# Two pairs of heads share the mapping and summing of their last 64 tokens, zeros fill idle TensorE for longer, and a regular block is written last

## The chip, the cores and the metric

The kernel runs on one core of a Trainium2 chip. A core has five engines that run side by side and meet at semaphores: TensorE (PE, matrix products into PSUM), VectorE (DVE), ScalarE (ACT), GpSimd (POOL) and SyncE (SP, which here issues all DMAs). PSUM has 8 banks of 512 fp32 columns. The metric is the time of one execution in microseconds.

## The reference, cut to what matters

Three stages follow each other: linear attention with an exponential feature map, a gated convolution with two dense layers, and a gMLP with a spatial product.

```python
# q, k, v: (8, 8, 576, 64), w_phi: (64, 128)
def phi(x):
    proj = einsum('bhsd,df->bhsf', x, w_phi)
    proj = proj - max(abs(proj), axis=-1, keepdims=True)
    return concatenate([exp(proj), exp(-proj)], axis=-1)
q_p, k_p = phi(q), phi(k)
kv  = einsum('bhsf,bhsd->bhfd', k_p, v)
z   = sum(k_p, axis=2)
num = einsum('bhsf,bhfd->bhsd', q_p, kv)
den = einsum('bhsf,bhf->bhs', q_p, z)[..., None] + 1e-06
x   = num / den                      # to (8, 576, 512)
# stage 2: gate = sigmoid(causal conv of x, 5 taps); x = (gate * (x @ w_val)) @ w_out
# stage 3: h = relu(x @ w_in); u, v = halves of h; v normalized over its 512 columns;
#          out = (u * (w_spatial @ v + b_spatial)) @ w_out2
```

## The kernel before, in words

Attention works on 32 pairs of heads (8 batches of 4 pairs). A pair's 128 partitions hold two heads of 64 channels. Its 576 tokens are 512 = 4 x 128 and a tail of 64.

For each pair, `load_k` loads the keys (128x576), the values of 512 tokens, and the values of the tail in two loads, one for each head. `project_k` maps the 512 tokens' keys (the keys are the stationary side, `w_phi` the moving one; both heads run at once on 64 rows of the array each). `project_q` maps the queries and, ahead of them, tokens 448 to 575 of the keys, of whose result only the last 64 rows are used. `kexp` and `kexp_last` take the maximum of the magnitudes and the two exponentials. `kvacc` sums the products of key features and values over tokens: two column tiles of 64 at once for the 512 tokens, then four 64x64 tiles at once for the tail. Each value row carries a column of ones, so the sums of the features come with it (65 columns). `kvout` copies the sums to SBUF. `qmax` takes the maximum over the feature partitions on POOL, `qexp` the exponentials, `weigh` (from the sixth pair on) folds the two halves of the denominator, `num` makes numerators and denominators in four column tiles of 32, and `divide` sends the denominators through DRAM (`rden`), spreads them and multiplies.

`mlp(b)` does the other stages for one batch: values (`val`), convolution and gate, the normalized half (`vchunk`), the other half (`uhalf`), the spatial product (`spatial`) and the output rows (`outrows`). All products there are three fp32r products of high and low parts. The tails of two batches (64 tokens each) share one block of output rows, which the kernel writes in two DMAs.

The order isn't the program's own. Every step is recorded as an operation with a key (a due time, in batches; pairs are 2/8 apart), and `Plan.order` simulates the engines with costs written into the kernel and takes, on each engine, the ready operation with the smallest key. A change of the array's form (full, 64 rows, 64 columns, 32 columns, 64x64) is charged by `MODE`. The constants `AK_...`, `AQ_...`, `W_...` and `M_...` shift the keys of the steps, `WINDOW`, `FA_HOLD` and `RA_HOLD` bound how far an operation may run ahead. Two arenas of SBUF columns (`fa` plain fp32, `ra` fp32r) and the 8 banks are given out along this order; an operation waits until there is room. Where PE is idle in the plan before `FILL` us and a bank has rested, a product of zeros is put in. The resulting order is fixed at build time, and each engine runs its instructions in it.

In the profile, L423 is the line through which all DVE and ACT instructions go, L458 POOL's, L469 the DMAs', L483 the MLP's products (`gemm`), L494 attention's products and the folding of weights (`products`), and L396 the zeros. The program records each fp32 product as two instructions.

Of the kernel before, what the change touches and what calls it, by code (L numbers as in the profile page):

```python
# [14 lines left out]
ACTF = mybir.ActivationFunctionType  # L15
ALU = mybir.AluOpType
# [4 lines left out]
F = 128  # L21
DM = 512
# [6 lines left out]
HALF = S // 2  # L29
TSPLIT = ((0, 256), (256, 320))  # L30
COLS = 29888
FA_COLS = 18368
A_LEAD, A_RATE = 1.6098, 1.0
AK_FIRST, AK_LOAD, AK_PROJ, AK_ACC, AK_SUM, AK_TURN = 2.1681, -0.1666, -0.9481, -1.1792, -0.0975, 0.5005
AQ_LOAD, AQ_PROJ, AQ_MAX, AQ_EXP, AQ_NUM, AQ_HEAD, A_DIV = -0.1281, -3.1984, -0.6423, 0.825, -0.9895, 1.7889, 5.0169
W_VAL, W_CONV, W_OUT, W_G, W_U, W_SP, W_OUT2, W_STEP = -1.0763, -1.0716, -1.6199, -1.783, -1.2251, -0.0604, 0.0451, 0.1666
M_CONV, M_VAL, M_V, M_U, M_SP, M_OUT, M_ALL = -0.2041, -0.309, -0.2989, -0.0525, 0.0418, 0.2823, 57.899
LONG_W, LONG_A, LONG_M = False, False, True
WINDOW = 0.5957
FA_HOLD = 2874  # L40
RA_HOLD = 3444
PA_HOLD = 0
LATER = 0.2441

MODE = 0.2916

EARLY = 5

REST, SOON = 6.0, 150.0
READY = {"PE": 1.0, "ACT": 2.0, "DVE": 0.9, "POOL": 0.6, "SP": 0.75}  # L50
# [12 lines left out]
FLOW, LAND, AFLOAT = 3.9, {"in": 1.4, "out": 0.3, "own": 0.85}, 8  # L63


FILL, RESTED = 60.0, 1.5


class View:
# [303 lines left out]
def attn_moe_gmlp_kernel(  # L373
# [88 lines left out]
    def dma(out, in_, queues=16):  # L462
        shape = out.shape() if isinstance(out, View) else out.shape
        packets = 1
        for d in shape[:-1]:
            packets *= d

        def run():
            nc.sync.dma_start(out=real(out), in_=real(in_))  # L469

        kind = "own" if views(in_) and views(out) else "in" if views(out) else "out"
        if kind == "own" and (in_.buf.dram or out.buf.dram):
            kind = "in" if in_.buf.dram else "out"
        moving = packets * (0.008 + 4 * shape[-1] / 27e3) / queues
        plan.add({"SP": (0.475 if shape[0] == 128 else 0.65, moving, run)}, views(in_), views(out), dma=kind)
# [14 lines left out]
    def products(t, mms, *modes):  # L490

        def run():
            for o, l, r, first, last in mms:
                nc.tensor.matmul(real(o), lhsT=real(l), rhs=real(r), start=first, stop=last)  # L494


        begun = {id(o.buf) for o, _, _, first, _ in mms if first}
        plan.add({"PE": (t, 1.0, run)}, [v for _, l, r, *_ in mms for v in (l, r)] +
                 [o for o, *_ in mms if id(o.buf) not in begun], [o for o, *_ in mms], (modes[0], modes[-1]))

    def psum():
        return pa.buf(512)
# [130 lines left out]
    def load_k(P):  # L633
        b, hp = divmod(P, NP)
        k, v, vr = fa.buf(S), fa.buf(4 * 2 * VW), fa.buf(VW)
        dma(k, kT[b, hp, :, 0:S])
        dma(v.rearrange("p (c d) -> p c d", c=4), v1[b, 0:REM, hp].rearrange("(c p) d -> p c d", p=128))
# [17 lines left out]
        ], ROWS)  # L655
        return kas

    def project_q(k, q):

        qas, rest = ([psum() for _ in range(2)] for _ in range(2))  # L660
        products(2 * 4 * (REM + F + S - REM) / 4800 + 0.13, [
            (rest[hh][:, 0:F], k[half(hh), S - 128:S], wphi[half(hh)], True, True) for hh in range(2)
        ] + [
            (rest[hh][:, F:F + 64], wphi[half(hh)], q[half(hh), REM:S], True, True) for hh in range(2)
        ] + [(qas[hh], wphi[half(hh)], q[half(hh), 0:REM], True, True) for hh in range(2)], ROWS)
        return [r[64:128, 0:F] for r in rest], [(qas[hh], rest[hh][:, F:F + 64]) for hh in range(2)]

    def kexp(acc, n):

# [9 lines left out]
    def kexp_last(accs):  # L679

        m, e = fa.buf(4)[64:128], fa.buf(2 * F)
        for hh, acc in enumerate(accs):
            dve("tensor_reduce", out=m[:, hh:hh + 1], in_=acc, axis=AX.X, op=ALU.max, apply_absolute_value=True)
        dve("tensor_scalar", out=m[:, 2:4], in0=m[:, 0:2], scalar1=-1.0, scalar2=None, op0=ALU.mult)
# [6 lines left out]
    def kvacc(kp, kpl, v, vr):  # L691


        accs, mms = [psum() for _ in range(2)], []
        for hh, acc in enumerate(accs):
            for c in range(4):
                for s in range(2):
                    for j in range(2):
                        mms.append((
                            acc[64 * j:64 * j + 64, DZ * s:DZ * s + DZ],  # L700
                            kp[hh][:, s, F * c + 64 * j:F * c + 64 * j + 64],
                            v[:, 2 * VW * c:2 * VW * c + 2 * VW][:, vcols(hh)], c == s == 0, False,
                        ))
        for s in range(2):
            for j in range(2):
                for hh, acc in enumerate(accs):
                    mms.append((acc[64 * j:64 * j + 64, DZ * s:DZ * s + DZ], kpl[half(hh), s, 64 * j:64 * j + 64],
                                vr[half(hh), hh:hh + DZ], False, s == 1))
        products((4 * 4 + 2) * 4 * DZ / 2400 + 0.3, mms, COLS2, TILES)
        return accs  # L710

    def kvout(accs):

        kv = fa.buf(4 * DZ)
        for hh, acc in enumerate(accs):
            copy(kv[:, 2 * DZ * hh:2 * DZ * hh + 2 * DZ], acc[:, 0:2 * DZ])
        return kv

    def values(kv, s, hh, i):
        o = 2 * DZ * hh + DZ * s + hh + 32 * i  # L720
# [71 lines left out]
    def attention():  # L792
        n = B * NP

        def at(t, sub=0.0):
            plan.key = (t + sub) / 8 * A_RATE - A_LEAD

        for P in range(n):
            t = 2 * P
            first = AK_FIRST if P == 0 else 0.0  # L800
            at(t, AK_LOAD - first)
            k, v, vr = load_k(P)
            at(t, AQ_LOAD - first)
            q = load_q(P)
            at(t, AK_PROJ - first)
            kas = project_k(k)
            at(t, AQ_PROJ - first)
            kls, qas = project_q(k, q)
            at(t, AK_ACC)
            kp = [kexp(a, 4) for a in kas]  # L810
            kpl = kexp_last(kls)
            at(t, AQ_MAX)
            pms = [qmax(a) for a in qas]
            at(t, AK_SUM)
            kva = kvacc(kp, kpl, v, vr)
            at(t, AK_TURN)
            kv = kvout(kva)
            es, ts = [], []
            for hh in range(2):
                at(t, AQ_HEAD * hh + AQ_EXP)  # L820
                es.append(qexp(*pms[hh]))
                at(t, AQ_HEAD * hh + AQ_NUM)
# [3 lines left out]
            at(t, A_DIV)  # L826
            divide(P, nd, dn)


    zrem = []  # L830

    def mlp(b):
# [148 lines left out]
        def outrows(z, places):  # L981
# [4 lines left out]
            copy(ot, acc)  # L986
            n = 128 // len(places)
            for i, (c, t0) in enumerate(places):
                dma(out[c, t0:t0 + n], ot[n * i:n * i + n])

        def outblock(j, o):
            outrows([[t[:, o:o + 128] for t in z] for z in zs[j]], [(b, TSPLIT[j][0] + o)])


        for j in range(2):
# [68 lines left out]
```

## Time and profile before

| | |
|---|---|
| median of 3 runs | 838.4 us (838.19 to 838.61) |
| profiled execution | 836.76 us, its span 835.0 us |
| mean granted clock of TensorE | 0.998 |
| PE busy | 816.7 us, 8240 products |
| DVE, ACT, POOL busy | 653.9, 533.9, 146.7 us |

The span is the time from the first to the last instruction; what the execution takes beyond it lies around it. Busy time of PE is that of overlapping products, so a full row of it doesn't yet say that each product is at its shortest; from one form's first start to the next form's first start is the safer measure. Idle time of an engine costs something only where that engine ends last.

### The profile page before, as it was taken

The page shows a single profiled execution, that of the slowest core. Times are in us where ns is not written, and L with a number is a line of the kernel's source. Part 1 is how long each engine was busy: PE and PEld are TensorE (multiplying, and loading weights), DVE is VectorE, ACT ScalarE, POOL GpSimd, SP SyncE. Part 2 cuts the span into 40 slices and gives each one's busy share as a digit, 9 for nine tenths or more (in the row PEclk, how much of TensorE's full clock was granted, in tenths as well). Part 3 has the DMA queues.
Part 4 walks back from the last instruction along what each step waited for, and adds up shares of the span by engine and source line. Part 5 has one row for each costly group of instructions (what it writes and reads, how often), then busy time and mean ns, then how long its engine had stood idle before and what let it go on. Part 6 is the DMA issues. An engine that isn't in the chain of part 4 may idle for free.

```text
span 835.0 us, 20782 instructions
## 1 busy us (share of the span) xinstructions
PE 816.7 (98%) x8240; PEld 684.1 (82%) x8240; DVE 653.9 (78%) x1583; ACT 533.9 (64%) x1148; POOL 146.7 (18%) x106
## 2 busy tenths in 40 slices
PE   9999699999999999999999999999999999999997
PEld 8455497789888888789788898889888897899896
DVE  5979899999879968598679968699587976586631
ACT  6868868986568647786468745678377754643321
POOL 3224222231213202231013202222022302000000
PEclk9999999999999999999999999999999999999999
DMA  8444513231222202321023212312023210110101
GB/s 289 123 160 142 135 61 117 89 100 40 74 62 73 72 28 62 100 74 57 18 87 90 72 40 59 96 53 72 28 72 92 74 42 29 46 30 13 38 7 64
DMA packets 55479, 62.23 MB, mean 75 GB/s; under 512 B 18259, under 2 KB 34771, under 8 KB 55381
## 3 DMA queue, kind: packets, MB, share of 16 engines
q1 hardware_dynamic: 55380, 60.90, 25.0%
q8 instruction: 65, 1.06, 0.6%
q14 instruction: 34, 0.27, 0.1%
HBM read 50.09 MB, written 9.58 MB: 71 GB/s over the span
## 4 chain that ended last, share of the span: by engine, by line
PE 77%; DVE 9%; ACT 6%; DMA 3%; issue 2%; SPq 1%; POOL 0%; ACTq 0%; DVEq 0%; POOLq 0%
PE bank L483 55%; PE bank L494 22%; DVE fa L423 7%; ACT fa L423 5%; DVE ra L423 1%; DMA fa<-rden 1%; SPq L469 1%; DMA fa<-in_w_spT_dram 1%; DMA fa<-in_w_in_dram 1%; DMA fa<-in_qT_dram 0%; DMA fa<-in_w_val_dram 0%; DMA rden<-fa 0%; ACT ra L423 0%; DVE wg L423 0%; POOL fa L458 0%
## 5 line engine op out<-in xcount | busy, mean ns | idle before, releaser
L423 ACT ACTIVATE fa<-fa 128x576 f32<-128x576 f32 (+3 forms) x413 | 260.5, 682 | 76.6 <-DVE fa L423 66.3
L423 ACT ACTIVATE fa<-bank 128x512 f32<-128x512 f32 (+6 forms) x342 | 132.5, 430 | 141.7 <-PE bank L483 94.9
L458 POOL PARTITION_ALL_REDUCE fa<-fa x64 | 141.9, 2259 | 356.8 <-ACT fa L423 185.1
L494 PE MATMUL bank<-fa 128*64 128x65 f32 (+2 forms) x3728 | 182.5, 286 | 7.5 <-ACT fa L423 6.0
L494 PEld LDWEIGHTS bank<-fa 128*64 128x64 f32 (+2 forms) x3728 | 117.2, 130 | 71.4 <-issue 25.4
L423 ACT ACTIVATE ra<-fa 128x256 fp32r<-128x256 f32 (+5 forms) x208 | 88.8, 462 | 61.5 <-DVE fa L423 31.7
L423 DVE TENSOR_TENSOR ra<-fa,ra 128x256 fp32r<-128x256 f32 (+4 forms) x256 | 109.5, 458 | 9.9 <-ACT ra L423 4.7
L483 PE MATMUL bank<-ws,ra 128*128 128x256 f32 (+1 forms) x768 | 114.2, 298 | 0.2 <-ACT fa L423 0.2
L423 DVE TENSOR_TENSOR fa<-fa 128x576 f32<-128x576 f32 (+2 forms) x240 | 98.7, 417 | 13.2 <-DMA fa<-rden 8.1
L483 PE MATMUL bank<-ra,wu 128*128 128x256 f32 (+1 forms) x768 | 106.9, 297 | 1.3 <-ACT fa L423 1.3
L483 PEld LDWEIGHTS bank<-ra,wu 128*128 128x128 f32 x768 | 104.2, 190 | 4.2 <-ACT fa L423 1.6
L483 PEld LDWEIGHTS bank<-ws,ra 128*128 128x128 f32 x768 | 105.4, 190 | 1.9 <-ACT fa L423 0.8
L483 PE MATMUL bank<-wg,ra 128*128 128x512 f32 x448 | 106.3, 392 | 0.1
L483 PE MATMUL bank<-ra,wv 128*128 128x256 f32 (+1 forms) x768 | 105.4, 297 | 0.1
L483 PEld LDWEIGHTS bank<-ra,wv 128*128 128x128 f32 x768 | 103.8, 191 | 1.6 <-DVE fa L423 0.7
L423 DVE SCALAR_TENSOR_TENSOR fa<-fa,convw 128x576 f32<-128x576 f32 x128 | 102.5, 820 | 2.0 <-ACT fa L423 1.8
L483 PE MATMUL bank<-wo,ra 128*128 128x512 f32 x432 | 101.9, 390 | 0.0
L423 DVE SCALAR_TENSOR_TENSOR fa<-fa 128x2 f32<-128x2 f32 (+3 forms) x192 | 87.1, 471 | 15.3 <-ACT fa L423 12.6
L483 PEld LDWEIGHTS bank<-wg,ra 128*128 128x128 f32 x448 | 83.1, 188 | 17.8 <-ACT fa L423 0.3
L483 PEld LDWEIGHTS bank<-wo,ra 128*128 128x128 f32 x432 | 80.2, 188 | 15.8
L423 DVE TENSOR_REDUCE fa<-bank 64x1 f32<-64x128 f32 (+1 forms) x128 | 57.4, 487 | 9.4 <-PE bank L494 7.9
L494 PEld LDWEIGHTS bank<-wphi,fa 64*128 64x128 f32 x640 | 44.1, 190 | 24.5 <-issue 11.1
(55 smaller groups left out, 561.8 us busy)
## 6 DMA issues: line engine op xcount, KB each, us to landing
fa<-in_kT_dram SPq DMA_DIRECT2D x32, 288.0 KB
fa<-in_qT_dram SPq DMA_DIRECT2D x32, 288.0 KB
fa<-rden SPq DMA_DIRECT2D x64, 144.0 KB
fa<-in_v_dram SPq DMA_DIRECT2D x32, 264.0 KB
out_dram<-fa SPq DMA_DIRECT2D x32, 256.0 KB
fa<-in_w_in_dram SPq DMA_DIRECT2D x8, 512.0 KB
fa<-in_w_outT_dram SPq DMA_DIRECT2D x4, 512.0 KB
fa<-in_w_val_dram SPq DMA_DIRECT2D x4, 512.0 KB
```

Of the source, the lines that this page charges most:

```text
L423: return lambda: getattr(engine, method)(**{k: real(v) for k, v in kw.items()})
L458: getattr(nc.gpsimd, method)(*(real(a) for a in args), **{k: real(v) for k, v in kw.items()})
L469: nc.sync.dma_start(out=real(out), in_=real(in_))
L483: nc.tensor.matmul(real(acc), lhsT=real(l), rhs=real(r), start=first and i == 0, stop=last and i == n - 1)
L494: nc.tensor.matmul(real(o), lhsT=real(l), rhs=real(r), start=first, stop=last)
```

## The change

From the fifth pair on (`ALONE` = 4), two pairs go together. Their key tails are loaded into the two halves of one 128x128 tile (64 tokens of each), their value tails into the two halves of the rows of another. `project_q` of the first pair maps no tail; that of the second maps both tails of both heads at once. `kexp_tails` works on 128 rows instead of 64. `kvacc` of the first pair does the 512 tokens only; that of the second also sums both tails, its own into its own banks and the first pair's into a third bank, and `kvadd` adds that to the first pair's sums on DVE. The keys of the first pair's query side are later by `AQ_LATE`. Zeros are put into idle PE until 110 us of the plan, not 60. The last batch's block of the two batches' tails goes ahead of its last regular block, and the very last copy is split between ACT and DVE. `fa` is 1280 columns wider and `ra` as much narrower, and the constants of the plan are others.

```diff
-FA_COLS = 18368
+FA_COLS = 19648
-AK_FIRST, AK_LOAD, AK_PROJ, AK_ACC, AK_SUM, AK_TURN = 2.1681, -0.1666, -0.9481, -1.1792, -0.0975, 0.5005
-AQ_LOAD, AQ_PROJ, AQ_MAX, AQ_EXP, AQ_NUM, AQ_HEAD, A_DIV = -0.1281, -3.1984, -0.6423, 0.825, -0.9895, 1.7889, 5.0169
+AK_FIRST, AK_LOAD, AK_PROJ, AK_ACC, AK_SUM, AK_TURN = 2.3372, -0.1253, 1.057, -0.9415, -0.9235, 1.7
+AQ_LATE = 1.8184
+AQ_LOAD, AQ_PROJ, AQ_MAX, AQ_EXP, AQ_NUM, AQ_HEAD, A_DIV = 0.027, -3.3025, -0.3784, 0.9397, -0.4381, 1.3614, 4.2184
...
-WINDOW = 0.5957
-FA_HOLD = 2874
-RA_HOLD = 3444
+WINDOW = 0.5475
+FA_HOLD = 3680
+RA_HOLD = 2576
-LATER = 0.2441
-MODE = 0.2916
-EARLY = 5
+LATER = 0.3125
+MODE = 0.3209
+EARLY, ALONE = 5, 4
-FILL, RESTED = 60.0, 1.5
+FILL, RESTED = 110.0, 1.5
...
+        if tails:
+            k, (kt, vr), i = fa.buf(REM), tails, P % 2
+            dma(kt[:, 64 * i:64 * i + 64], kT[b, hp, :, REM:S])
+            dma(k, kT[b, hp, :, 0:REM])
+            load_v()
+            dma(vr[half(i)], v1[b, REM:S, hp], queues=8)
+            return k, v, vr
...
-            (rest[hh][:, 0:F], k[half(hh), S - 128:S], wphi[half(hh)], True, True) for hh in range(2)
+        mms = [] if keys is None else [(rest[hh][:, 0:F], keys[half(hh)], wphi[half(hh)], True, True) for hh in range(2)]
...
+        if tails:
+            kps, vr = tails
+            accs.append(psum())
+            for s in range(2):
+                for hh in range(2):
+                    for j in range(2):
+                        for i in range(2):
+                            acc, o = (accs[hh], DZ * s) if i else (accs[2], 2 * DZ * hh + DZ * s)
+                            mms.append((acc[64 * j:64 * j + 64, o:o + DZ], kps[hh][half(i), s, 64 * j:64 * j + 64],
+                                        vr[half(i), vcols(hh)], i == s == hh == 0, s == 1 and i + hh > 0))
+            n = 4
+        products((4 * 4 + n) * 4 * DZ / 2400 + (0.3 if n else 0.08), mms, COLS2, *([TILES] if n else []))
...
+    def kvadd(kv, acc):
+        dve("tensor_tensor", out=kv, in0=kv, in1=acc[:, 0:4 * DZ], op=ALU.add)
...
+        for P in range(ALONE):
+            pms, kv, _ = keys(P, None, 1)
+            queries(P, pms, kv, 0.0)
+        for P in range(ALONE, n, 2):
+            tails = fa.buf(128), fa.buf(2 * VW)
+            pms, kv, _ = keys(P, tails, 0)
+            pms2, kv2, kva = keys(P + 1, tails, 1)
+            kvadd(kv, kva[2])
+            queries(P, pms, kv, AQ_LATE)
+            queries(P + 1, pms2, kv2, 0.0)
...
+            if end:
+                act(ot[:, 0:DM // 2], acc[:, 0:DM // 2])
+                dve("tensor_copy", out=ot[:, DM // 2:DM], in_=acc[:, DM // 2:DM])
+            else:
+                copy(ot, acc)
...
         outblock(1, 0)
-        outblock(1, 128)
         if b % 2:
             outrows(zrem, [(b - 1, REM), (b, REM)])
             zrem.clear()
+        outblock(1, 128)
```

## Rows read from the trace of the kernel before

**Rows 1.** The page: PE's busy time (share, instructions); granted clock in 40 slices.

```profile
PE 816.7 (98%) x8240; PEld 684.1 (82%) x8240; DVE 653.9 (78%) x1583; ACT 533.9 (64%) x1148; POOL 146.7 (18%) x106
...
PEclk9999999999999999999999999999999999999999
```

**Rows 2.** Windows: stretch, length, then busy us (and instructions) by engine, clock, DMA.

```profile
60.00:106.00 46.00, 38.08 (x592) 24.23 (x590) 42.31 (x75) 39.96 (x89) 13.20 (x10) 0.98 0.50 132
106.00:172.60 66.60, 64.41 (x640) 54.84 (x638) 65.74 (x155) 54.04 (x116) 18.45 (x10) 0.99 0.27 84
172.60:830.50 657.90, 657.34 (x6438) 567.93 (x6438) 503.47 (x1279) 396.56 (x856) 98.69 (x68) 1.00 0.21 58
```

**Rows 3.** Waits of PE, 172.6 to 830.5 us: total us, times, longest.

```profile
PE bank L494 <- ACT fa L423: 0.3, 1, 0.3
```

**Rows 4.** Chain that ended last, 100 to 180 us, shares by engine and line.

```profile
by line: DVE fa L423 51.3%; ACT fa L423 18.2%; DVE ra L423 11.4%; PE bank L483 5.0%; issue 4.4%; PE bank L494 4.3%; DVE ws L423 1.7%; ACT ra L423 1.6%; DVE wo L423 1.5%; ACT wo L423 0.8%; DVEq L423 0.0%
```

**Rows 5.** Timeline of PE, one visit: start, us, engine, line, out<-in, shape, count.

```profile
352.26 2.15 PE L494 MATMUL bank<-fa 128*32 128x288 f32 x32
...
354.82 2.48 PE L494 MATMUL bank<-fa 128*64 128x65 f32 x80
357.23 0.49 PE L494 MATMUL bank<-wphi,fa 64*128 64x128 f32 x4
357.56 1.25 PE L494 MATMUL bank<-fa,wphi 64*128 64x64 f32 x8
358.64 1.06 PE L494 MATMUL bank<-wphi,fa 64*128 64x128 f32 x16
359.63 0.74 PE L483 MATMUL bank<-ws,ra 128*128 128x256 f32 x4
```

**Rows 6.** Timeline of PE, the tail's products of the same visit.

```profile
356.84 0.46 PE L494 MATMUL bank<-fa 64*64 64x65 f32 x16
```

**Rows 7.** Windows, two neighbouring stretches inside the tail's products.

```profile
356.94:357.00 0.06, 0.06 (x8) 0.06 (x12) 0.06 (x1) 0.06 (x1) 0.00 (x0) 1.00 0.15 10
357.00:357.06 0.06, 0.06 (x12) 0.06 (x12) 0.06 (x1) 0.06 (x1) 0.00 (x0) 1.00 0.06 4
```

**Rows 8.** Groups by form on PE, 172.6 to 830.5 us: count, busy us, mean ns.

```profile
L494 PE MATMUL bank<-fa,wphi 64*128 64x512 f32 x88 | 23.8, 617 | 0.0
...
L494 PE MATMUL bank<-fa 64*64 64x65 f32 x368 | 10.6, 230 | 0.0
```

**Rows 9.** Groups by form on DVE, whole span.

```profile
L423 DVE SCALAR_TENSOR_TENSOR fa<-fa,convw 128x576 f32<-128x576 f32 x128 | 102.5, 820 | 2.0 <-ACT fa L423 1.8
...
L423 DVE TENSOR_REDUCE fa<-bank 64x1 f32<-64x128 f32 x64 | 16.2, 291 | 1.2
...
L423 DVE TENSOR_TENSOR fa<-fa,bank 128x256 f32<-128x256 f32 x32 | 13.0, 415 | 10.1 <-PE bank L483 9.9
L423 DVE TENSOR_SCALAR fa<-fa 64x2 f32<-64x2 f32 x32 | 12.3, 385 | 1.0
```

**Rows 10.** Groups by form on ACT, whole span.

```profile
L423 ACT ACTIVATE fa<-bank,fa 64x128 f32<-64x128 f32 x128 | 39.8, 357 | 9.7 <-DVE fa L423 8.4
...
L423 ACT ACTIVATE fa<-bank 128x256 f32<-128x256 f32 x20 | 7.5, 383 | 9.2 <-PE bank L483 7.0 <-DVE fa L423 2.0
```

**Rows 11.** Windows, the stretch with the low granted clock.

```profile
100.00:110.00 10.00, 7.46 (x91) 7.06 (x92) 8.37 (x12) 8.77 (x19) 2.33 (x2) 0.83 0.60 174
```

**Rows 12.** Groups by form on PE, whole span: the products of zeros.

```profile
L396 PE MATMUL bank<-zero 128*128 128x128 f32 x88 | 13.1, 312 | 1.0 <-POOL zero L458 1.0
```

**Rows 13.** Timeline, the last two blocks' copy and writes (SPq: SP's DMA issue).

```profile
828.45 0.33 SPq L469 DMA_DIRECT2D out_dram<-fa  x1
...
830.54 0.60 ACT L423 ACTIVATE fa<-bank 128x512 f32<-128x512 f32 x1 [2.12 <-PE bank L483]
831.16 1.16 SPq L469 DMA_DIRECT2D out_dram<-fa  x2
```

**Rows 14.** Windows, the data of the last two blocks on the DMA engines (last columns).

```profile
829.20:830.00 0.80, 0.80 (x5) 0.68 (x4) 0.00 (x0) 0.00 (x0) 0.00 (x0) 1.00 0.84 328
...
832.20:833.70 1.50, 0.00 (x0) 0.00 (x0) 0.00 (x0) 0.00 (x0) 0.00 (x0) 1.00 0.75 175
```

More of the change, by code (lines that the diff above doesn't have):

```diff
@@ L31 @@
 COLS = 29888
[L32 to L37 removed]
+FA_COLS = 19648
+A_LEAD, A_RATE = 1.6067, 1.0
+AK_FIRST, AK_LOAD, AK_PROJ, AK_ACC, AK_SUM, AK_TURN = 2.3372, -0.1253, 1.057, -0.9415, -0.9235, 1.7
+AQ_LATE = 1.8184
+AQ_LOAD, AQ_PROJ, AQ_MAX, AQ_EXP, AQ_NUM, AQ_HEAD, A_DIV = 0.027, -3.3025, -0.3784, 0.9397, -0.4381, 1.3614, 4.2184
+W_VAL, W_CONV, W_OUT, W_G, W_U, W_SP, W_OUT2, W_STEP = -1.2738, -0.7798, -1.837, -1.8381, -0.9694, -0.3728, 0.0709, 0.1637
+M_CONV, M_VAL, M_V, M_U, M_SP, M_OUT, M_ALL = -0.2929, -0.4488, -0.1986, 0.0546, -0.1458, 0.261, 57.899
 LONG_W, LONG_A, LONG_M = False, False, True
[L39 to L41 removed]
+WINDOW = 0.5475
+FA_HOLD = 3680
+RA_HOLD = 2576
 PA_HOLD = 0
[L43 to L47 removed]
+LATER = 0.3125
+MODE = 0.3209
+EARLY, ALONE = 5, 4
 REST, SOON = 6.0, 150.0
@@ L631, in vcols, with load_k, load_v @@
         return slice((2 * VW - DZ) * hh, (2 * VW - DZ) * hh + DZ)
-    def load_k(P):
+    def load_k(P, tails=None):
         b, hp = divmod(P, NP)
-        k, v, vr = fa.buf(S), fa.buf(4 * 2 * VW), fa.buf(VW)
+        v = fa.buf(4 * 2 * VW)
+        def load_v():
+            dma(v.rearrange("p (c d) -> p c d", c=4), v1[b, 0:REM, hp].rearrange("(c p) d -> p c d", p=128))
+        if tails:
[5 more added lines that the diff above has]
+            return k, v, vr
+        k, vr = fa.buf(S), fa.buf(VW)
         dma(k, kT[b, hp, :, 0:S])
-        dma(v.rearrange("p (c d) -> p c d", c=4), v1[b, 0:REM, hp].rearrange("(c p) d -> p c d", p=128))
+        load_v()
         for hh in range(2):
@@ L656, in project_k, with project_q @@
         return kas
-    def project_q(k, q):
+    def project_q(q, keys):
         qas, rest = ([psum() for _ in range(2)] for _ in range(2))
-        products(2 * 4 * (REM + F + S - REM) / 4800 + 0.13, [
-            (rest[hh][:, 0:F], k[half(hh), S - 128:S], wphi[half(hh)], True, True) for hh in range(2)
-        ] + [
+        mms = [] if keys is None else [(rest[hh][:, 0:F], keys[half(hh)], wphi[half(hh)], True, True) for hh in range(2)]
+        products(2 * 4 * ((F if mms else 0) + S) / 4800 + 0.13, mms + [
             (rest[hh][:, F:F + 64], wphi[half(hh)], q[half(hh), REM:S], True, True) for hh in range(2)
         ] + [(qas[hh], wphi[half(hh)], q[half(hh), 0:REM], True, True) for hh in range(2)], ROWS)
-        return [r[64:128, 0:F] for r in rest], [(qas[hh], rest[hh][:, F:F + 64]) for hh in range(2)]
+        return [r[:, 0:F] for r in rest], [(qas[hh], rest[hh][:, F:F + 64]) for hh in range(2)]
     def kexp(acc, n):
@@ L681, in kexp_last @@
         m, e = fa.buf(4)[64:128], fa.buf(2 * F)
-        for hh, acc in enumerate(accs):
-            dve("tensor_reduce", out=m[:, hh:hh + 1], in_=acc, axis=AX.X, op=ALU.max, apply_absolute_value=True)
-        dve("tensor_scalar", out=m[:, 2:4], in0=m[:, 0:2], scalar1=-1.0, scalar2=None, op0=ALU.mult)
+        accs = [a[64:128] for a in accs]
+        shifts(m, accs)
         for hh, acc in enumerate(accs):
@@ L689, in kexp_last, with shifts, kexp_tails, kvacc @@
         return e.rearrange("p (s x) -> p s x", s=2)
-    def kvacc(kp, kpl, v, vr):
+    def shifts(m, accs):
+        for hh, acc in enumerate(accs):
+            dve("tensor_reduce", out=m[:, hh:hh + 1], in_=acc, axis=AX.X, op=ALU.max, apply_absolute_value=True)
+        dve("tensor_scalar", out=m[:, 2:4], in0=m[:, 0:2], scalar1=-1.0, scalar2=None, op0=ALU.mult)
+    def kexp_tails(accs):
+        m, es = fa.buf(4), [fa.buf(2 * F) for _ in range(2)]
+        shifts(m, accs)
+        for hh, acc in enumerate(accs):
+            for s in range(2):
+                act(es[hh][:, F * s:F * s + F], acc, ACTF.Exp, scale=1.0 - 2.0 * s,
+                    bias=m[:, 2 + hh - 2 * s:3 + hh - 2 * s])
+        return [e.rearrange("p (s x) -> p s x", s=2) for e in es]
+    def kvacc(kp, v, last=None, tails=None):
         accs, mms = [psum() for _ in range(2)], []
@@ L701, in kvacc @@
                             kp[hh][:, s, F * c + 64 * j:F * c + 64 * j + 64],
-                            v[:, 2 * VW * c:2 * VW * c + 2 * VW][:, vcols(hh)], c == s == 0, False,
-                        ))
[L704 to L709, printed above, removed]
+                            v[:, 2 * VW * c:2 * VW * c + 2 * VW][:, vcols(hh)], c == s == 0,
+                            c == 3 and s == 1 and not last and not tails,
+                        ))
+        n = 0
+        if last:
+            kpl, vr = last
+            for s in range(2):
+                for j in range(2):
+                    for hh, acc in enumerate(accs):
+                        mms.append((acc[64 * j:64 * j + 64, DZ * s:DZ * s + DZ], kpl[half(hh), s, 64 * j:64 * j + 64],
+                                    vr[half(hh), hh:hh + DZ], False, s == 1))
+            n = 2
+        if tails:
+            kps, vr = tails
+            accs.append(psum())
+            for s in range(2):
+                for hh in range(2):
+                    for j in range(2):
+                        for i in range(2):
[4 more added lines that the diff above has]
+        products((4 * 4 + n) * 4 * DZ / 2400 + (0.3 if n else 0.08), mms, COLS2, *([TILES] if n else []))
         return accs
@@ L714, in kvout @@
         kv = fa.buf(4 * DZ)
-        for hh, acc in enumerate(accs):
+        for hh, acc in enumerate(accs[:2]):
             copy(kv[:, 2 * DZ * hh:2 * DZ * hh + 2 * DZ], acc[:, 0:2 * DZ])
         return kv
+    def kvadd(kv, acc):
+        dve("tensor_tensor", out=kv, in0=kv, in1=acc[:, 0:4 * DZ], op=ALU.add)
     def values(kv, s, hh, i):
@@ L796, in at, with keys @@
             plan.key = (t + sub) / 8 * A_RATE - A_LEAD
-        for P in range(n):
+        def keys(P, tails, i):
             t = 2 * P
             first = AK_FIRST if P == 0 else 0.0
+            late = 0.0 if i else AQ_LATE
             at(t, AK_LOAD - first)
-            k, v, vr = load_k(P)
-            at(t, AQ_LOAD - first)
+            k, v, vr = load_k(P, tails)
+            at(t, AQ_LOAD - first + late)
             q = load_q(P)
@@ L806, in attention, with queries @@
             kas = project_k(k)
-            at(t, AQ_PROJ - first)
-            kls, qas = project_q(k, q)
+            at(t, AQ_PROJ - first + late)
+            kls, qas = project_q(q, k[:, S - 128:S] if not tails else tails[0] if i else None)
             at(t, AK_ACC)
             kp = [kexp(a, 4) for a in kas]
-            kpl = kexp_last(kls)
-            at(t, AQ_MAX)
+            last, both = None, None
+            if not tails:
+                last = kexp_last(kls), vr
+            elif i:
+                both = kexp_tails(kls), vr
+            at(t, AQ_MAX + late)
             pms = [qmax(a) for a in qas]
             at(t, AK_SUM)
-            kva = kvacc(kp, kpl, v, vr)
+            kva = kvacc(kp, v, last, both)
             at(t, AK_TURN)
-            kv = kvout(kva)
+            return pms, kvout(kva), kva
+        def queries(P, pms, kv, late):
+            t = 2 * P
             es, ts = [], []
             for hh in range(2):
-                at(t, AQ_HEAD * hh + AQ_EXP)
+                at(t, AQ_HEAD * hh + AQ_EXP + late)
                 es.append(qexp(*pms[hh]))
-                at(t, AQ_HEAD * hh + AQ_NUM)
+                at(t, AQ_HEAD * hh + AQ_NUM + late)
                 if P >= EARLY:
@@ L825, in attention @@
             nd, dn = num(es, kv, ts)
-            at(t, A_DIV)
+            at(t, A_DIV + late)
             divide(P, nd, dn)
+        for P in range(ALONE):
[8 more added lines that the diff above has]
+            queries(P + 1, pms2, kv2, 0.0)
     zrem = []
@@ L979, in spatial, with outrows @@
                 split(z[:, 256:320], *(t[:, 64 * (b % 2):64 * (b % 2) + 64] for t in zrem[m]))
-        def outrows(z, places):
+        def outrows(z, places, end=False):
             spent(2.56, M_OUT)
@@ L985, in outrows @@
             gemm(acc, [t for k in range(KD) for t in three(z[k][0], z[k][1], wo[0][k], wo[1][k])])
-            copy(ot, acc)
+            if end:
[3 more added lines that the diff above has]
+                copy(ot, acc)
             n = 128 // len(places)
@@ L991, in outblock @@
         def outblock(j, o):
-            outrows([[t[:, o:o + 128] for t in z] for z in zs[j]], [(b, TSPLIT[j][0] + o)])
+            outrows([[t[:, o:o + 128] for t in z] for z in zs[j]], [(b, TSPLIT[j][0] + o)], b == B - 1 and j == 1 and o == 128)
         for j in range(2):
```

## The prediction

> **What bounds the kernel now.** I read the page's engine shares first, then a table of stages, then PE's waits, then one stretch of instructions in order of time.
>
> TensorE (PE) is busy for 98% of the span (the table above), at the full granted clock in every slice [rows 1]. That share alone proves little, since zeros fill its gaps at the start, so it has to be split by stage. From 172.6 to 830.5 us PE works 657.34 of 657.90 us, while VectorE (DVE) works 503 and ScalarE (ACT) 397 [rows 2]; PE idles for 0.6 us, and its longest wait is 0.3 [rows 3]. In this stretch time is PE work and nothing else. From 106 to 172.6 us it is different: PE idles 2.2 us and DVE only 0.9 [rows 2], and half of the chain that ends last runs over DVE's line for `fa` [rows 4]. From 60 to 106 us PE is idle for 7.9 us [rows 2]. So an edit is worth PE time in the long stretch, DVE time before it, and latency after the last product.
>
> In the long stretch attention comes as visits, one per pair of heads, between blocks of the MLP [rows 5]: numerators and denominators from 352.26, the key-value sums from 354.82, the mapping of the last keys (rest) from 357.23, that of the queries from 357.56, that of the keys from 358.64, and at 359.63 the MLP goes on. 7.37 us in all.
>
> **The change, part by part.** I take times from one start to the next, because shown durations overlap.
>
> *Tails summed together.* The 16 instructions on 64x64 tiles, the tail of one pair, begin at 356.84 [rows 6] and the next form at 357.23 [rows 5]: 0.39 us. Two neighbouring stretches of 0.06 us hold 8 and then 12 instructions [rows 7]; none has ended, so four begin per 0.06 us, and 16 take 0.24. The other 0.15 is the change of form, the first products behind it included. Of two pairs the first now has no tail (-0.39) and the second has 32 instructions, four waves more (+0.24): 0.15 us less. 368 such instructions come after 172.6 us [rows 8], which is 23 pairs or 11.5 double pairs: 11.5 x 0.15 = 1.7 us. Bounds: nothing, and 0.39 per double pair (4.5 us) if the longer tail cost no more than the short one.
>
> The Trainium skill ("TensorE: Matmul & The Clock Gate", "Wait — 56ns, not 53.3ns?" in Part 1) says that starts of matmuls are never under about 25 ns apart however small they are. By it 32 instructions take twice what 16 take and this edit gives nothing. The trace speaks against it for four tiles side by side (four starts in 0.06 us [rows 7]), though 16 in 0.39 us is 24 ns apiece.
>
> *Last keys mapped together.* Of two pairs one loses its four rest instructions. They hold 0.33 us (357.23 to 357.56), but a part of that is the change of form, which the query products inherit. The 16 key products of the same kind take 0.99 us [rows 5], so four are worth 0.25; bounds 0.2 and 0.33. 88 long query products after 172.6 us [rows 8] are 22 pairs: 11 x 0.25 = 2.7 us.
>
> *Exponentials, maxima and the added sum.* Per double pair DVE did four reductions of 0.25 us (16.2/64) and two small scalings of 0.385 [rows 9]: 1.8 us. Now it does half of that, plus one addition of 260 columns out of PSUM, by the nearest row 0.42 [rows 9]: 1.3. That is 0.5 us less. ACT does four exponentials of 0.31 us (39.8/128 [rows 10]) less, 1.2 us. After 172.6 us both lie beside PE and count nothing. Before it, where DVE ends last, 32-23 = 9 pairs are summed, five of them from the fifth pair on: 2.5 x 0.5 = 1.2 us less. Bounds: a loss of 2.2 (other keys give the start another order, and PE idles twice as long) and a gain of 3.9 (the 2.2 us idle, and 1.7 of half clock, below).
>
> *A new wait.* The first pair's numerators now wait for the addition, and that for the second pair's sums. On PE everything behind the numerators would wait too, on DVE what stands behind the addition. What covers it: the first pair's query side is moved back by `AQ_LATE`, 1.8 of the 2.0 units between pairs, and in a visit numerators stand ahead of sums [rows 5], so that sums of one visit meet numerators in a later one, 7 us or more on. I take 0; without that cover it is the rival below.
>
> *Loads.* Per pair there were loads of k, v and two of the v tail; now k tail, k, v and one v tail. The count on SP's queue stays, k itself goes out one issue later (0.33 us by the nearest row [rows 13]), against a lead of some us: 0. Bounds: one issue either way, once, at the start.
>
> *Longer zeros.* From 100 to 110 us the mean granted clock is 0.83 [rows 11], that is 1.7 us lost at 1.2 GHz. Zeros until 110 us of the plan should keep 2.4 GHz there, as the clock stayed at 1.00 while zeros filled the earlier gaps [rows 1, 12]. But DVE ends last in that stage, so I count 0; bounds: a gain of 1.7, and a loss of 2.5 (a zero product of 0.31 us [rows 12] ahead of a real one, eight times).
>
> *Arenas.* `ra` shrinks by 1280 columns, `fa` grows by as many. I count 0, since PE hardly waits [rows 3]; a new wait as long as the 0.3 there, once per batch, would be 2 us; `fa` room can also save that.
>
> *A regular block last.* Before, the last copy took 0.60 us, and two writes were issued from 831.16 on [rows 13], with their data going out until 833.7 [rows 14]: 2.5 us. The regular block before it was issued at 828.45 [rows 13] and was out by 830.0 [rows 14]: 1.55. So 1.0 less. Half of the copy takes 0.42 on DVE (256 columns out of PSUM [rows 9]), ACT's half beside it: 0.2 less. Sum 1.2; bounds 0.5 and 1.4.
>
> **Sum.** 1.7 + 2.7 + 1.2 + 1.2 = 6.8 us. The profiled execution took 836.76 us (span 835.0 and 1.76 around it): 830.0. The median of the runs, 838.4, lies 1.64 above it, so the forecast is 831.6.
>
> **The rivals.**
>
> 1. *Two pairs share a visit.* With the queries of both pairs due at nearly the same time, forms could be entered once for both. Each change of form costs 0.15 us; a visit has four and the way back. If two are saved per double pair, 14 x 0.30 = 4.2 us more: 827.4; all four, 823.2. For it: the keys of the first pair's queries move next to the second's. Against it: one visit's products already fill up to 4 of the 8 PSUM banks with the queries alone, and two pairs' would fill all.
>
> 2. *Visits split.* The first pair's keys keep their time while its queries move, so its visit may fall into two. Each extra visit costs two changes of form, 0.30 us. One per double pair is 4.2 us (835.8); with 1.5 per double pair 6.3 of 6.8 us are gone: 837.9, no change. Against it: the planner charges a change of form, and a little more than before.
>
> 3. *The starts floor.* If 25 ns per start holds, 1.7 us fall away: 833.3.
>
> 4. *PE waits for the added sum (slower).* Place: the first pair's numerators, once per double pair. Price: 0.42 us of addition, one DVE instruction of up to 0.82 ahead of it in the queue (a step of the convolution [rows 9]), so about 1.0 us: 11.5 x 1.0 = 11.5, less the gain of 6.8: +4.7, 843.1. It decides from 0.6 us per double pair on. For it: it is the one wait that is really new, and PE takes its work in order. Against it: numerators stand first in a visit.
>
> That the tails aren't merged, so that the change does nothing, can't be: the loops write them so. Only the start and the end could be all that is left (2.4 us, 836.0).
>
> **Chances.** Forecast 0.50 (its own range 829 to 834.5), shared visits 0.18, split visits 0.13, the floor 0.06, the new wait 0.13. About 0.2%, 1.7 us, is what a measurement can tell from no change. Faster: 0.50 + 0.18 + 0.06, and 0.04 of the split visits, 0.78. Same (836.7 to 840.1): 0.07 of the split visits and 0.03 of a small wait, 0.10. Slower: 0.02 + 0.10 = 0.12. The range 825.5 to 838.5 leaves out the new wait's upper part, the deepest shared visits and the worst split ones, some 0.18 together; it holds the bounds of start, zeros and arenas taken one at a time.
>
> **What would show it.** Tails: 512 instructions on 64x64 tiles as before, but 32 at a time from the fifth pair on, 0.63 us from start to start, not 0.78. Rest: about 0.25 us less in every second visit. Sum: PE busy after its last start-up wait lower by some 4 us at the same 1.00 clock, with PE's waits still under 1 us. Start: the last DVE-bound piece of the chain ends about 1 us earlier; clock 1.00 around 104. End: a single write, and about 3.3 us instead of 4.5 from the last product to the end of the span. Wrong would be: PE waits for DVE at the numerators (rival 4), more than one way into the tiled forms per pair (2), or fewer (1).

## The result, and the profile after

The changed kernel takes 823.8 us (median of 4 runs, 823.13 to 825.26) against 838.3 before: 0.983 of it, 95% interval 0.9813 to 0.9847. The forecast was 831.6, the range 825.5 to 838.5. The direction was right and the gain twice what was forecast: 14.5 us, not 6.8. In the two profiled executions it is 12.7 us (836.76 to 824.03) and in their spans 12.8 (835.0 to 822.2). The spans are what the following splits up.

The page after, PE's row and the granted clock, which answer to [rows 1]; the share of the span stands in brackets:

```profile
PE 812.2 (99%) x8242; PEld 687.9 (84%) x8242; DVE 641.7 (78%) x1570; ACT 512.1 (62%) x1078; POOL 143.2 (17%) x106
...
PEclk9999999999999999999999999999999999999999
```

The group of the zeros after, which answers to [rows 12]:

```profile
L397 PE MATMUL bank<-zero 128*128 128x128 f32 x146 | 21.4, 306 | 1.7 <-POOL zero L459 1.0 <-ACT fa L424 0.7
```

These rows give the first reading. Before, PE was busy for 816.7 us, 13.1 of it on zeros: 803.6 us of real work, and 31.4 us of the span without any (18.3 idle, 13.1 zeros). After, 812.2 less 21.4 is 790.8, and 10.0 idle with 21.4 of zeros is 31.4 again. So the whole 12.8 us are real work of PE. What PE lacks in all, most of it at the start, is as much as before, with more zeros and less idle time in it. (Busy times are modelled and hold overlaps, so these differences are good to some tenths.)

The stretches of [rows 2], after. The last one ends 0.8 us behind the last product (818.23):

```profile
60.00:106.00 46.00, 44.56 (x530) 31.84 (x523) 41.85 (x76) 36.46 (x78) 10.77 (x6) 1.00 0.45 134
106.00:172.60 66.60, 65.39 (x731) 53.83 (x730) 59.97 (x158) 52.10 (x114) 17.75 (x12) 1.00 0.29 86
172.60:819.00 646.40, 644.32 (x6381) 562.21 (x6379) 495.21 (x1257) 378.70 (x797) 96.54 (x68) 1.00 0.21 58
```

PE is still what bounds the long stretch: 1.3 us of its idle time there lie before the last product, the longest wait 0.5. In the middle one DVE is no longer full: 6.6 us idle, where it had 0.9 before.

Where the work went shows in the timeline of PE over two visits, which answers to [rows 5] (start, us, line, shapes, count):

```profile
205.23 2.15 PE L495 MATMUL bank<-fa 128*32 128x288 f32 x32
207.19 0.67 PE L495 MATMUL bank<-fa,ones 128*32 128x288 f32 x8
207.68 2.12 PE L495 MATMUL bank<-fa 128*32 128x288 f32 x32
209.62 0.67 PE L495 MATMUL bank<-fa,ones 128*32 128x288 f32 x8
210.22 1.35 PE L495 MATMUL bank<-fa,wphi 64*128 64x64 f32 x8
211.40 0.39 PE L495 MATMUL bank<-wphi,fa 64*128 64x128 f32 x4
211.62 1.25 PE L495 MATMUL bank<-fa,wphi 64*128 64x64 f32 x8
212.71 1.95 PE L495 MATMUL bank<-wphi,fa 64*128 64x128 f32 x32
214.59 3.03 PE L484 MATMUL bank<-wg,ra 128*128 128x512 f32 x12
...
228.58 4.58 PE L495 MATMUL bank<-fa 128*64 128x65 f32 x160
233.09 1.19 PE L484 MATMUL bank<-wg,ra 128*128 128x512 f32 x4
```

There are still two visits for two pairs, but each does one side for both: first the numerators of both and the mapping of both (205.23 to 214.59, 9.36 us), 14 us later the sums of both (228.58 to 233.09, 4.51 us). A form is entered once for two pairs. Together that is 13.87 us, where two visits of 7.37 were 14.74: 0.87 us less per double pair, 12.2 for 14 of them if all went so. The long stretch repeats it: wherever two pairs are together, their numerators take 4.99 us where one pair's took 2.56, their sums 4.51 where one pair's took 2.41, their mapping 4.37 to 4.50 where one pair's mostly took 2.40. In the whole trace all 14 double pairs share their numerators and ten their sums; the sums of the other four fall into two visits, three of these before 185 us. So it is somewhat less than 12.2.

The tail's burst in the same trace, which answers to [rows 6] (the first line), with the next product behind it:

```profile
232.46 0.70 PE L495 MATMUL bank<-fa 64*64 64x65 f32 x32
233.09 0.50 PE L484 MATMUL bank<-wg,ra 128*128 128x512 f32 x1
```

32 instructions in 0.63 us from start to start, as worked out, and not 0.78 or 0.80: 20 ns apiece, so the floor on starts (rival 3) doesn't hold for these tiles side by side.

### The profile page after: what moved, and what is told of

Read it like the earlier page. It is cut to its first block, busy times and chain, and to the rows that moved or that the text cites. A ratio compares the mean times of both kernels' runs of the same rounds, so it can differ in the third digit from the quotient of the medians.

```text
span 822.2 us, 20683 instructions
## 1 busy us (share of the span) xinstructions
PE 812.2 (99%) x8242; PEld 687.9 (84%) x8242; DVE 641.7 (78%) x1570; ACT 512.1 (62%) x1078; POOL 143.2 (17%) x106
## 5 line engine op out<-in xcount | busy, mean ns | idle before, releaser
L424 ACT ACTIVATE fa<-fa 128x576 f32<-128x576 f32 (+3 forms) x413 | 256.7, 678 | 80.4 <-DVE fa L424 68.3
L459 POOL PARTITION_ALL_REDUCE fa<-fa x64 | 138.3, 2225 | 365.4 <-ACT fa L424 227.9
L495 PE MATMUL bank<-fa 128*64 128x65 f32 (+3 forms) x3728 | 176.7, 284 | 0.4 <-DVE fa L424 0.4
L495 PEld LDWEIGHTS bank<-fa 128*64 128x64 f32 (+3 forms) x3728 | 116.5, 130 | 53.8 <-issue 18.6
L424 ACT ACTIVATE ra<-fa 128x256 fp32r<-128x256 f32 (+4 forms) x208 | 88.6, 458 | 73.8 <-DVE fa L424 44.4
L484 PE MATMUL bank<-wg,ra 128*128 128x512 f32 x448 | 108.2, 393 | 0.0
L424 DVE TENSOR_TENSOR fa<-fa 128x576 f32<-128x576 f32 (+2 forms) x240 | 94.0, 398 | 8.9 <-DMA fa<-rden 5.4
L424 DVE SCALAR_TENSOR_TENSOR fa<-fa 128x2 f32<-128x2 f32 (+3 forms) x192 | 85.4, 458 | 14.2 <-ACT fa L424 11.4
L424 DVE TENSOR_REDUCE fa<-bank 128x4 f32<-128x512 f32 (+2 forms) x100 | 50.9, 540 | 17.7 <-PE bank L495 10.2
L424 DVE TENSOR_TENSOR fa<-fa,bank 128x256 f32<-128x256 f32 (+2 forms) x78 | 34.8, 446 | 31.8 <-PE bank L495 13.9
```

The source lines that it names most:

```text
L424: return lambda: getattr(engine, method)(**{k: real(v) for k, v in kw.items()})
L459: getattr(nc.gpsimd, method)(*(real(a) for a in args), **{k: real(v) for k, v in kw.items()})
L484: nc.tensor.matmul(real(acc), lhsT=real(l), rhs=real(r), start=first and i == 0, stop=last and i == n - 1)
```

## The experiments

| kernel | us | to the kernel before (95%) | PE's real work | zeros and idle |
|---|---|---|---|---|
| before | 838.3 | | 803.6 | 31.4 |
| changed | 823.8 | 0.983 (0.9813 to 0.9847) | 790.8 | 31.4 |
| changed, once more | 822.9 | 0.9829 (0.9812 to 0.9846) | 790.4 | 33.0 |
| x1_other_form | 827.6 | 0.9878 (0.9861 to 0.9896) | 796.4 | 29.1 |
| x2_same_form | 822.6 | 0.9819 (0.9802 to 0.9837) | 790.6 | 29.9 |
| x3_first_pair_again | 831.6 | 0.9931 (0.9918 to 0.9945) | 799.8 | 31.2 |
| e1_no_late | 906.1 | 1.0816 (1.0791 to 1.0841) | 817.5 | 86.7 |
| e4_merge_only | 907.3 | 1.0829 (1.0793 to 1.0865) | 823.1 | 79.7 |
| e8_late_old_keys | 839.7 | 1.0038 (1.0023 to 1.0053) | 800.4 | 37.6 |
| e2_late_unmerged | 855.9 | 1.0232 (1.0216 to 1.0247) | 809.3 | 44.6 |
| e9_late_one_key | 838.9 | 1.0018 (1.0008 to 1.0028) | 800.7 | 36.1 |
| e10_key_zeros110 | 838.5 | 1.0012 (0.9998 to 1.0026) | 792.2 | 44.8 |
| e11_start_keys | 828.6 | 0.9886 (0.9863 to 0.9909) | 792.3 | 34.8 |
| e3_zeros_60 | 821.1 | 0.9813 (0.9794 to 0.9831) | 791.5 | 26.0 |
| e5_one_copy | 822.5 | 0.9835 (0.9819 to 0.9852) | 789.2 | 30.2 |
| v_zeros60_one_copy | 820.1 | 0.9796 (0.9783 to 0.9809) | 792.0 | 26.3 |

The last two columns are from the page of each kernel's profiled execution, worked out as above. The kernel before was 836.3 to 838.3 us over the chips used, so compare ratios.

**x1_other_form and x2_same_form: what a change of form costs.** A tiny product behind each pair's numerators, in another form or in theirs, with every other instruction where it was. The cut shows x1; x2 appends `(acc[0:32, 448:449], ones, wphi[:, 0:1], True, True)` in its place:

```diff
-        products(len(mms) * HALF / 2400 * 1.01, mms, COLS4)
+        cost = len(mms) * HALF / 2400 * 1.01
+        if ts:
+            mms.append((acc[0:64, 448:449], wphi[0:64, 0:64], wphi[0:64, 0:1], True, True))
+        products(cost, mms, COLS4)
```

> The changed kernel with one tiny product (one column, on a 64x64 tile) written behind the numerators of each pair from the sixth on (27 of them); nothing else moves in any engine's order. It parts the numerators of two pairs in one visit, and these from the mapping: three more changes of form per double pair, some 41 in all. Theory A (a visit shared by two pairs is worth what its saved changes of form cost, 0.15 us each): 41 x 0.15 = 6.2 us plus the products, 823.8 + 6 to 8 = 830 to 832. Rival B (the gain lies in fewer products and in the start, a change of form costs next to nothing): within 1 us of 823.8 and of x2_same_form.

> The same 27 tiny products, but in the numerators' own form (32 columns), so that no form changes. Both theories: 27 x 2 instructions of at most 0.06 us, 0.5 to 3 us over the changed kernel: 824.3 to 826. Under A x1_other_form lies 5 to 6 us above this one, under B beside it.

x2 is no slower than the changed kernel (I expected 0.5 to 3 us more), and x1 is 5.0 us above x2: 0.12 us for each of some 41 changes of form (40 in the trace). In PE's real work the two lie 5.8 us apart, 0.145 for each. x1's own time is 2.4 us under the range of theory A, but it lies 5 us above x2, as A has it: A holds, at four fifths of its price or a little more. A visit of x1, timeline of PE:

```profile
203.12 2.15 PE L495 MATMUL bank<-fa 128*32 128x288 f32 x32
205.08 0.67 PE L495 MATMUL bank<-fa,ones 128*32 128x288 f32 x8
205.68 0.27 PE L495 MATMUL bank<-wphi 64*64 64x1 f32 x2
205.88 2.15 PE L495 MATMUL bank<-fa 128*32 128x288 f32 x32
```

The denominators (`ones`) start 0.80 us ahead of the next numerators here; in the changed kernel it is 0.49 (207.19 to 207.68). Two changes and the product between them cost 0.31 us.

**x3_first_pair_again: what the merged products are worth.**

```diff
-        mms = [] if keys is None else [(rest[hh][:, 0:F], keys[half(hh)], wphi[half(hh)], True, True) for hh in range(2)]
...
+        none = keys is None
+        mms = [(rest[hh][:, 0:F], (wphi if none else keys)[half(hh)], wphi[half(hh)], True, True) for hh in range(2)]
...
+        if not last and not tails:
+            for s in range(2):
+                for j in range(2):
+                    for hh, acc in enumerate(accs):
+                        mms.append((acc[64 * j:64 * j + 64, 256 + DZ * s:256 + DZ * s + DZ], wphi[half(hh), 64 * j:64 * j + 64],
+                                    wphi[half(hh), 0:DZ], True, True))
```

> The changed kernel in which each first pair does its own tail products again (16 instructions on 64x64 tiles and 4 of the mapping), on constant operands and into columns that nobody reads, with every engine's order otherwise the same. The prediction priced the first at 0.39 us and the second at 0.25: 14 x 0.64 = 9.0 us over the changed kernel (0.58 to 0.66 per double pair: 8 to 9.3). If small products cost nothing beside each other: under 4 us. That would take the merged products' share of the gain with it (14 x 0.40 = 5.6 us by the prediction's prices).

It takes 8.7 us more than the changed kernel on the same chip, 0.62 per double pair. So the two prices, 0.39 and 0.25, were right in their sum; neither was tried alone. They aren't products only: the first pair's tail now stands between the sums of two pairs, and the trace has 149 runs of one form on PE where the changed kernel has 125 (zeros counted with the full form). With the 0.24 that the longer tail costs (0.63 against 0.39) the merged tails give 0.40 per double pair, 5.6 us in 14, of which 0.15 each is the change of form that a tail no longer needs.

**e1_no_late and e4_merge_only: the first pair's queries in their old place.** e1 is the changed kernel with

```diff
-AQ_LATE = 1.8184
+AQ_LATE = 0.0
```

and e4 has the changed code with all constants of before, the same 0.0 among them.

> The changed kernel with AQ_LATE = 0 (and 320 columns moved from fa to ra, without which its order finds no room). Merged tails stay, but the written order has 151 runs of one form on TensorE instead of 109: most visits belong to one pair again. Theory A: 42 x 0.15 = 6.3 us more, 829 to 832. Rival B: the products are the same, so 823 to 825.5.

> The changed code with every constant of the plan as before (AQ_LATE = 0, zeros until 60 us): merged tails, the new end, but the old keys. The written order has 149 runs of one form, 8 more than the kernel before. Theory A: products 14 x 0.36 = 5.0 us less, forms 8 x 0.15 = 1.2 more, the end 0.6 less: 838.3 - 4.4 = 834. Rival B (merging itself is what pays): 824 to 828.

Both theories missed by 70 us and more. PE waits in every part of the long stretch. For e4, stretch 200 to 800 us: PE's busy time in 600 us and mean clock 0.97, and the longest waits of PE (total us, times, longest):

```profile
200.00:800.00 600.00, 558.98 (x5559) 476.15 (x5552) 447.36 (x1088) 325.65 (x684) 97.46 (x66) 0.97 0.19 57
```

```profile
PE bank L495 <- ACT fa L424: 28.7, 14, 5.4
PE bank L484 <- ACT fa L424: 9.9, 11, 3.7
```

41 us idle, up to 5.4 at a time, most of it in attention's products behind exponentials, and half clock (1.2 GHz) around the longer gaps. It is rival 4's cause (the first pair's numerators need the second pair's sums), as far as the cure by lateness (e8, below) shows, but for the most part not in rival 4's place: in e4 24.9 of the 41 us are idle ahead of the sums and none ahead of the numerators. In e1 9.8 of 39.8 idle us in the same stretch are ahead of the numerators. My reading, argued from the planner's code: numerators that are due and cannot be ready are the oldest open operation, and `WINDOW` lets nothing due much later begin, so PE runs out of other work and then waits for the exponentials of the pair in hand.

**e8_late_old_keys and e2_late_unmerged.** e8 is e4 with `AQ_LATE = 1.8184`. e2 is the changed kernel with `keys(P, None, 0)` and `keys(P + 1, None, 1)`: late queries, nothing merged.

> As e4_merge_only (changed code, every constant of the plan as before, zeros until 60 us), but with the first pair's query side moved back by 1.8184. The written order has 120 runs of one form on TensorE, 29 fewer than e4 and 11 more than the changed kernel. Theory C (without the move the first pair's numerators, due but not ready, hold up everything due later: it is the move that lets two pairs go together): the 50 us of waits of e4 are gone and the time is 823.8 + 11 x 0.13 = 825 to 828. Rival D (the other retuned constants do it): it stays above 860.

> The changed kernel with the late queries of each first pair, but every pair maps and sums its own tail (nothing merged; 640 columns moved from fa to ra, without which its order finds no room). The written order has 153 runs of one form, 44 more than the changed kernel. Theory A (forms and products add up): 14 x 0.36 = 5.0 us of products and 44 x 0.13 = 5.7 us of forms more: 834 to 836. Rival (lateness alone shares the visits): 824 + 5 = 829. Rival D' (a first pair's sums that must wait for late queries stall TensorE as in e1): above 850.

The move alone takes some 66 us off e4 (by the ratios), so that in the long stretch PE is full again (e8, 200 to 800 us):

```profile
200.00:800.00 600.00, 596.49 (x5977) 513.95 (x5975) 469.60 (x1201) 354.64 (x752) 97.57 (x66) 1.00 0.20 58
```

That shows what the lateness is worth. But e8 stays 16 us above the changed kernel (17 by the ratios), where I expected 1 to 4. e2 came out at 856, in the range of its third theory, but only in part by its cause. PE's real work is 18.5 us above the changed kernel's, as theory A's products and 58 more runs of one form in the trace would have it together with a mean clock of 0.994, and zeros and idle time are 13 us more, about half of it before 200 us. That an unmerged first pair maps its tail together with its queries, so that late queries make its sums late, is how the code reads; no run shows that this is what the 13 us are.

In the orders that were run, merging without lateness lost 8% (e1, e4), lateness without merging 2% (e2), and both together gain only with the new constants (changed kernel against e8). The code of before with the new constants was not run, so what retuning would have given by itself stays open.

**e9_late_one_key, e10_key_zeros110 and e11_start_keys: what e8 lacks.** e9 is e8 with `AK_PROJ` 1.057; e10 is e9 with `FILL` 110; e11 is e9 with the changed kernel's `W_`, `AK_` and `AQ_` lines.

> As e8_late_old_keys (changed code, old constants, late queries), with one more constant of the change: the key of the mapping of keys later by 2.0 units (AK_PROJ 1.057). The written order then maps the keys of both pairs in the visit of their queries, as the changed kernel does, with 114 runs of one form (e8 120, changed 109). If this key is what clears the waits of e8 (10 us of idle TensorE behind the start): 825 to 829 where the changed kernel is 823. If the waits come from the other constants (holds, arenas, MLP keys): 834 to 840, as e8.

> e9_late_one_key with zeros until 110 us of the plan (121 runs of one form after the start's zeros are counted in). e9 lost 8.5 us of TensorE time to the half clock (mean clock 0.990 over its span, most of it before 190 us). If the longer zeros are what the start lacks: the clock near 0.998 and 6 to 8 us less than e9, 831 to 833. If the half clock falls behind the zeros' end, or zeros stand in the way of real work: 835 to 840.

> e9_late_one_key with the changed kernel's keys of the weights (W) and of all attention steps (AK, AQ); the MLP's keys, the holds, arenas, MODE, WINDOW and the zeros until 60 us as before. 108 runs of one form. If the waits of e8 and e9 between 30 and 190 us come from the order in which weights are folded and pairs are started: those waits fall from 15 us to 6 or less, and the time is 822 to 828. If they come from the MLP's keys or the holds: 834 to 840.

One key isn't enough. e10 cured the clock (0.997 instead of 0.990) and PE's real work fell by 8.5 us, but zeros rose by 12.4 and the time stayed. Two readings are left, its second expectation among them: PE doesn't end the start, so that its clock there costs nothing, or the zeros stood in the way of real products for as long as the clock gained. e3 and `v_zeros60_one_copy`, below, speak for the second. e11 recovers 10 of the 16 us, by its order in the start (its 2000th real product begins at 210.3 us, e9's at 219.5): its real work is 8.4 us under e9's (some 6 of it less half clock, at 0.997 instead of 0.990) and its zeros and idle 1.3 less. It lies 0.6 us above my range, and its waits fell less than I wrote (idle from 19.5 to 16.0 us, the end included). What holds the remaining 5 us back (MLP keys, holds, `MODE`, `WINDOW`) wasn't taken apart.

**e3_zeros_60, e5_one_copy and the two together.**

> The changed kernel with zeros only until 60 us of the plan, all else as it is. If the longer zeros give back the 1.7 us that the half clock took from TensorE: 825 to 826.5, with a stretch at 1.2 GHz near 90 to 105 us. If nothing there is bound by TensorE: 823.5 to 824.5, whatever the clock.

> The changed kernel with its last block copied out of PSUM by one engine, all else the same. In the trace of the changed kernel DVE's half (0.42 us) begins only when ACT's (0.38) has ended, 0.84 us from the first start to the last end against 0.60 for one whole copy: 0.2 us less, 823.6, hardly to be told from 823.8; its trace shows the end, from the last product to the last instruction, 0.2 us shorter. If the halves ran side by side in most executions it would be 0.2 us longer.

> The changed kernel with two of its parts undone that gave nothing or less alone: zeros until 60 us (e3: 0.9813) and one copy of the last block (e5: 0.9835, its end 0.2 us shorter). If the longer zeros cost some 1.5 us: 1.0 to 2.5 us under the changed kernel on this chip. If e3 was scatter: 0.2 us under it, not to be told.

Beside the last of them the changed kernel was timed once more on the same chip:

> The changed kernel itself once more, as the one to compare with on this chip: 0.983 of the kernel before, between 0.981 and 0.985, by its first runs.

It was 822.9. e3 and e5 can't be told from the changed kernel by their intervals; e3's 821.1 lies under both of its expectations. Together, in `v_zeros60_one_copy`, they give 820.1 us, 2.9 under the changed kernel on the same chip (0.9796, its interval just clear of that of 0.9829): the fastest version here, by 0.4 us more than I had expected. Its zeros and idle are 26.3 us instead of 31 to 33, its real work 1.2 more: the clock does fall once without the later zeros (0.50 from 87.0 to 90.4 us), and still the start is shorter. One copy is worth 0.2 of the 2.9, so the longer zeros seem to cost the changed kernel some 2.5 us, give or take 2. Its trace shows how they could: the later zeros run on until the next real product, which begins without an idle moment behind them (timeline of PE, changed kernel):

```profile
86.24 1.38 PE L397 MATMUL bank<-zero 128*128 128x128 f32 x10 [0.68 <-ACT fa L424]
87.55 2.40 PE L495 MATMUL bank<-fa 128*64 128x65 f32 x64
89.88 2.27 PE L397 MATMUL bank<-zero 128*128 128x128 f32 x18
92.09 1.16 PE L495 MATMUL bank<-wphi,fa 64*128 64x128 f32 x16
```

The end of the changed kernel, timeline (ACT's half, DVE's half, and SP's write):

```profile
818.32 0.38 ACT L424 ACTIVATE fa<-bank 128x256 f32<-128x256 f32 x1 [2.12 <-PE bank L484]
818.74 0.42 DVE L424 COPY fa<-bank 128x256 f32<-128x256 f32 x1 [12.69 <-ACT fa L424]
```

```profile
819.19 0.34 SPq L470 DMA_DIRECT2D out_dram<-fa  x1
```

The same in e5, with one copy:

```profile
815.74 0.60 ACT L424 ACTIVATE fa<-bank 128x512 f32<-128x512 f32 x1 [2.12 <-PE bank L484]
```

```profile
816.36 0.34 SPq L470 DMA_DIRECT2D out_dram<-fa  x1
```

Two halves one behind the other take 0.87 us from the copy's start to the write; one copy takes 0.62.

## Why the prediction was wrong

The step that failed is the sum's assumption that a visit stays what it was, one pair's, so that only the merged tails and last keys count on PE and shared forms stand at nothing. What the runs showed in its place: two pairs share their visits, 34 changes of form fall away beside those of the tails, and at 0.12 to 0.145 us each they give 4 to 5 us. The prediction named the other case (rival 1, two pairs share a visit, 827.4 with half the changes saved and 823.2 with all) and gave it 0.18, because two pairs' queries alone would fill PSUM. That argument failed: the timeline shows both pairs' numerators and mappings back to back without a wait. That 823.8 us is so near the end of that rival is partly luck: it asks for four changes per double pair beyond the sum, 56 in all, and 34 came, which at its 0.15 would be 826.5. The rest came from terms that the sum had at nothing or too small, less two that it had too large.

Point by point, with the profiled executions' 12.8 us:

- Merged tails and last keys, forecast 4.4 us after 172.6: right in price (x3: 0.62 us where 0.64 was written; tail burst 0.63). For all 14 double pairs it is 5.6.
- Shared forms, forecast 0: a change of form is 0.12 us in time and 0.145 in PE's real work (x1 against x2; 0.15 had been written). A double pair took ten, two visits with five each, and takes six, three in each of two visits, where all is shared. One of the four is the tail's, which the 0.40 of the merged tails holds already; the three others are what is left of the 0.87 in the timeline, 0.47. Not all double pairs go so: the traces have 173 runs of one form before and 125 after (zeros counted with the full form), 48 fewer, 14 of them tails. The 34 others are 4.1 us at 0.12 and 4.9 at 0.145.
- Half clock, forecast 0 with a bound of 1.7: it is gone from the trace (1.00 from 100 to 110 us), and PE's real work should be less by that much. No run shows that the time gained by it: in e10 it stayed, and without the longer zeros the kernel was faster (`v_zeros60_one_copy`).
- Start, forecast 1.2 from DVE's savings: PE's slack (zeros and idle) is 31.4 us before and after, so nothing is left of it in the account. DVE did get room (6.6 us idle from 106 to 172.6).
- End, forecast 1.2: from the last product (818.23 by the windows) to the end of the span about 4.0 us, where it had been 4.5: 0.5. The single write gave 0.8 where 1.0 was forecast (issue at 819.19, span's end 3.0 later, against 831.16 and 3.8), and the split copy lost 0.25 instead of winning 0.2.
- The new wait, cost 0 thanks to `AQ_LATE`: right, and the cover is worth 66 us (e4 against e8). Rival 4's price of 1.0 us per double pair was far too small for what happens without it.
- That the constants are neutral was assumed without a word. They are not: the same code with the old ones and the lateness (e8) is 0.4% slower than the kernel before. So the gain belongs to code and constants together.

The first three sum to 5.6 + 4.1 + 1.7 = 11.4 us of real work, 12.2 at the higher price of a change, against 12.8 measured. The rest, about 1 us, isn't assigned. Nor are 1.8 of the 14.5 us between the medians, which the profiled executions don't show.

## What to carry to other kernels

Where a tensor engine is full and its array changes form often, count the changes per unit of work before and after an edit, beside the products: here the 48 that fell away were worth 5.8 to 7.0 us, the products that were removed 3.5 (14 x 0.25). When an edit makes one item wait for the next one, its due time in the planner is part of the edit; without it the same code was 8% slower (e4 against e8). Filling idle TensorE kept its clock here (mean 0.997 instead of 0.990 in e10), but no run got faster by the longer zeros, so such filling has to be tried by itself.

## What the runs showed of the hardware that was not expected

- Products on 64x64 tiles start 20 ns apart on average: 32 instructions in 0.63 us, the change of form included.
- A change of the array's form costs about 0.12 us (5.0 us for some 41), though only one tiny product is done in between; 27 products of one column in the form at hand cost nothing that the times show (x2, 0.9819 against 0.983).
- ACT and DVE copying the two halves of one bank came one after the other: DVE's half started 0.04 us after ACT's had ended. Whether the bank or the order of writes to the common output tile made it wait wasn't tried.
- Half clock in the start, cured by zeros, moved PE's real work by 8.5 us and the time by nothing (e9, e10).
